# A fused RWKV-6 and SiLU kernel: the first layer of units 3 to 11 by eleven half-products in place of twelve

## The chip, the cores and the metric

The kernel runs on one core of a Trainium2 chip, everything in float32. The metric is the time on the device in microseconds, the median over runs. Engines are called TensorE (PE; PEld is its weight load), VectorE (DVE), ScalarE (ACT), GpSimd (POOL) and SyncE (SP, which issues the DMAs).

## The reference

An attention block of the RWKV-6 kind is followed by two matrix products with a SiLU between them:

```python
batch, n_heads, seq, head_dim = (4, 8, 768, 48)
for t in range(S):
    kt, vt, rt, wt = (k[:, :, t], v[:, :, t], r[:, :, t], w[:, :, t])
    cur = np.einsum('bhd,bhe->bhde', u[None] * kt, vt)
    y[:, :, t] = np.einsum('bhd,bhde->bhe', rt, state + cur)
    state = wt[:, :, :, None] * state + np.einsum('bhd,bhe->bhde', kt, vt)
...
x = y.transpose(0, 2, 1, 3).reshape(B * S, H * D)      # 3072 x 384
h = x @ w_in                                           # 384 x 2048
g = h * (1.0 / (1.0 + np.exp(-h)))
out = g @ w_out                                        # 2048 x 384
```

## The kernel before

The work is cut into twelve units: 128 time steps (`L`) of two batches (`NB`), so 256 tokens (`TU`). Units 0, 2, 4 and so on hold batches 0 and 1, the others batches 2 and 3. A unit goes through the attention part, then the first layer, then the second layer.

**Attention.** Within a unit the recurrence is computed by levels of blocks that double in length (1, 2, 4 up to 64). `turn` transposes w, r and k into rows of time (VectorE, L356). `grow_keys` (GpSimd, L630) and `grow_queries` or `prepare` (VectorE, L612 and L767) multiply keys and queries by the decays of the blocks. `burst(i, l)` makes the score products of two levels at once on TensorE (L688), from the queries before and after a `prepare`. `keep_level` moves them into `score` (VectorE L706 for short blocks, ScalarE L788 for the long ones). `block_bonus` and `block_sum` compute the scores inside blocks of eight tokens on GpSimd (L487) and VectorE (L521), from the tile `tokens_rk`, which `load_rk` fetches. The sums go through DRAM (`block_move`: `kept`, then `spare`) and are spread by ScalarE (`block_spread`, L548 and L550) and written into `score` by VectorE (`block_write`, L557). After level 6, `go_on(i, 6)` multiplies the queries once more (L612). Then TensorE computes `turn_apart` (L807), `y_state` (L831, reads those queries, and L838), `y_values` (L852) and `update` (L892). `move_x` (L918) carries the result through ten DMAs into the tile `xt`, in three chunks of 128 input columns; there is one buffer of it.

**First layer.** `up(i, m)`, m from 0 to 7, multiplies `xt` by 256 columns of `w_in`: two blocks of 128 columns, three chunks each, with all 256 tokens as the moving side (L1000). ScalarE applies the SiLU from PSUM into `gt` (L1009).

**Second layer.** From unit 1 on it takes seven products of halves in place of eight (a scheme of Winograd's kind). `sums(i, m)` makes the four sums of `gt` on VectorE (L1048, tile `temps`), `quarter(i, which)` the seven products (L1066), with VectorE adding the parts from PSUM (L1075). `weight_sums` made the four sums of `w_out` once, early.

**Order.** All instructions are written in an order fixed by hand (`manual_schedule`); each engine works through its own in that order. From unit 3 on, one round of the main loop handles unit i's attention, unit i-1's first layer and unit i-2's second layer: `mix(i)` gives the attention in eleven groups (13 for i = 3), and `room` says how many steps of the layers follow each group. For i from 4 on it is

```python
steps = downs(i - 2) + ups(i - 1)          # 7 quarters, then 8 first-layer steps
room = (2, 1, 2, 2, 1, 1, 1, 2, 1, 1, 1)
```

So quarters 3 and 4 follow group 2 (key and query products of level 2), quarters 5 and 6 follow group 3 (`prepare(i, 3)`), and the first-layer steps follow group 4 (`burst(i, 3)`, block sums, `block_move`, `load_rk`) to group 10. Group 8 holds `burst(i, 5)`, `keep_level` 5 and 6 and `go_on(i, 6)`; group 9 the first four `block_bonus` steps of unit i+1; group 10 `turn_apart` to `update`, the transposes of unit i+1's w and k, and one of the four `sums`. `move_x(i - 1)` stands in group 1. After unit 11's attention, `downs(10)`, `ups(11)` and `downs(11)` follow with nothing between.

**Loads.** w, r and k of a unit are fetched by 16 DMAs each (`load_blocks`, L123) into `raw`, which has two slots, one for even and one for odd units. SP issues all DMAs of the kernel in their written order. In round i, r of unit i+1 and w and k of unit i+2 are fetched, spread over groups 2 to 10.

PSUM: `p_h` and `p_o` have two buffers each, `p_m` and `p_sc` two banks each.

Of the kernel before, what the change touches and what calls it, by code (L numbers as in the profile page):

```python
# [8 lines left out]
F32 = mybir.dt.float32  # L9
# [6 lines left out]
ALU = mybir.AluOpType  # L16
# [22 lines left out]
def kernel(  # L39
# [17 lines left out]
    NB = 2  # L57
# [56 lines left out]
    def load_blocks(i, name, g):  # L114


        n, b0 = units[i]
        src, t0 = {"w": w, "r": r, "k": k}[name], n * L + g * 32
        room = raw[:, i % NSLOT, WRK[name]].rearrange("p b h d -> p (b h d)").rearrange("p (q g d) -> p q g d", q=Q, d=32)
        for e in range(2):  # L120
            for a in range(2):
                d0, d1 = a * 32, min(D, a * 32 + 32)
                nc.sync.dma_start(out=room[(2 * e + a) * 32:(2 * e + a + 1) * 32, :, g, 0:d1 - d0],  # L123
                                  in_=src[b0:b0 + NB, e::2, t0:t0 + 32, d0:d1].rearrange("b q t d -> t (b q) d"))
# [217 lines left out]
    def turn(i, b, name):  # L342
        dst = {"w": tw, "r": tr, "k": tk}[name]
        if i not in dst:
            rows = NX if name == "k" else Q
            t = pt.tile([128, rows, L], F32, name="t" + name, bufs=2 if name == "r" else 1)
            dst[i] = [t] if name == "w" else t
        t = dst[i][0] if name == "w" else dst[i]
        if i < NTOK:
            if (i, b, name) not in turned:  # L350
                turn_in(i, b, name)
            turn_out(i, b, name, t)
        else:
            row0 = b * NP + (NP if name == "k" else 0)
            to, back = t[:, row0:row0 + NP, :], name == "k" and b == 1
            nc.vector.transpose(out=to[:, ::-1, ::-1] if back else to,  # L356
                                in_=raw[:, i % NSLOT, WRK[name], b].rearrange("p h d -> p (h d)"))

    turned = {}

# [569 lines left out]
    def mix(i):  # L930

        ahead = i + 1 < len(units)

        def at(now, *steps):
            return steps if now else ()

        def bonus_steps(j, *steps):
            return [(block_bonus, j, x) for x in steps]

        def sum_steps(j, *steps):  # L940
            return [(block_sum, j, x) for x in steps]

        def turns(j):
            return [*both(turn, j, "w"), (product, j, 0), *both(turn, j, "k")]

        def start(j):
            return [*[(product, j, l) for l in range(1, NL)], (grow_own, j, 1)]

        end = [[*at(ahead, *bonus_steps(i + 1, 0, 1, 2, 3))],
               [*at(i < len(units) - NB, (turn_apart, i), (turn_k, i)), (y_state, i), *both(y_values, i), *at(ahead, *turns(i + 1)),  # L950
                (sums, i - 1, FH // 2 - 2), *both(update, i), *at(not ahead, (move_x, i))]]
        if i < NPAIR:
            groups = [[*both(turn, i, "w"), (product, i, 0)],
                      [*both(turn, i, "k"), (odd_ones, i)], [*both(turn, i, "r"), (start_levels, i), (prepare_keys, i, 1)],
                      [(prepare, i, 1), *[(product, i, l) for l in range(1, NL)]],
                      [(burst, i, 1), (keep_level, i, 1)],
                      [(keep_level, i, 2), (go_on, i, 2)],
                      [(prepare, i, 3), (reverse_v, i), (bonus, i, 0), (bonus_sum, i, 0)],
                      [(bonus, i, 1), (burst, i, 3), (keep_level, i, 3), (bonus, i, 2)],
                      [(keep_level, i, 4), (go_on, i, 4), (bonus_sum, i, 1), (load_rk, i + 1), (load_u,)],  # L960
                      [(prepare, i, 5), (make_block_mask,), (bonus_spread, i), (bonus_write, i)],
                      [(burst, i, 5), (keep_level, i, 5), (keep_level, i, 6), (go_on, i, 6)], *end]
        else:
            groups = [[*both(turn, i, "r"), (grow_own, i, 0)], [*start(i), *sum_steps(i, 0, 1), *bonus_steps(i, 4, 5), (move_x, i - 1)],
                      [(odd_keys, i, 2), (grow_keys, i, 2, False), (grow_queries, i, 2), *sum_steps(i, 2)],
                      [(prepare, i, 3), *bonus_steps(i, 6, 7)],
                      [(burst, i, 3), (keep_level, i, 3), *sum_steps(i, 3, 4), (block_move, i), *at(ahead, (load_rk, i + 1))],
                      [(keep_level, i, 4), (go_on, i, 4)],
                      [(prepare, i, 5), (reverse_v, i)],
                      [(block_spread, i), (block_write, i)],  # L970
                      [(burst, i, 5), (keep_level, i, 5), (keep_level, i, 6), (go_on, i, 6)], *end]

        loads = [*at(i >= NPAIR - 1 and ahead, *block_loads(i + 1, "r")), *at(i + NSLOT < len(units), *block_loads(i + NSLOT, "wk"))]
        if i + 1 < len(units):
# [17 lines left out]
    FH, DH = FC // 2, DM // 2  # L992
    NFIRST = 2 * PW // (2 * TU)

    def up(i, m):
        p_h = ps.tile([128, 2, TU], F32, name="p_h", bufs=2)
        for a in range(2):
            f = 2 * m + a
            for c in range(KC):
                nc.tensor.matmul(p_h[:, a, :], lhsT=w_in_sb[:, c, f * 128:(f + 1) * 128], rhs=xt[i][:, c, :],  # L1000
                                 start=(c == 0), stop=(c == KC - 1))
# [7 lines left out]
        nc.scalar.activation(out=gt[i, m], in_=p_h, func=AF.Silu)  # L1009

    def out_room(b):

# [28 lines left out]

    def sums(i, m):

        lower, upper = (gt[i, x].rearrange("p a (b t) -> p b a t", b=NB) for x in (m, m + FH // 2))
        s1, s2, s3, s4 = (quarters[:, x, 2 * m:2 * m + 2, :] for x in range(4))
        for out, one, two, op in ((s1, lower[:, 1], upper[:, 1], ALU.add), (s2, s1, lower[:, 0], ALU.subtract),
                                  (s3, lower[:, 0], lower[:, 1], ALU.subtract), (s4, upper[:, 0], s2, ALU.subtract)):
            nc.vector.tensor_tensor(out=out, in0=one, in1=two, op=op)  # L1048

    ob, partial = {}, {}  # L1050
# [1 line left out]
    def quarter(i, which):  # L1052

        n, b0 = units[i]

        def g(b, half):
            return lambda f: gt[i, (f + half * FH) // 2][:, f % 2, b * L:(b + 1) * L]

        def s(x):
# [22 lines left out]

    def ups(i):

        steps = [[(up, i, m)] for m in range(FC // 2)]
# [92 lines left out]
    for step in downs(len(units) - 2) + ups(len(units) - 1) + downs(len(units) - 1):  # L1178
        do(*step)


# [28 lines left out]
```

## Time and profile before

| | |
|---|---|
| time, median of 3 runs | 595.06 us (594.48 to 595.62) |
| span of the profiled execution (its own time is given by this span alone) | 593.4 us, clock 1.000 |
| TensorE busy | 584.0 us (98%) |
| VectorE busy | 411.1 us (69%) |
| GpSimd busy | 351.6 us (59%) |
| ScalarE busy | 225.5 us (38%) |
| first layer, L1000, 1152 records | 259.1 us |
| quarters, L1066 (three groups, 1212 records) | 88.1 + 86.5 + 30.4 us |

A float32 matmul shows as two records, each with its own weight load. Busy time of a group of matmuls counts the time that at least one of them was under way; the time of one record is its latency, and the distance between the starts of two is what a record costs. In the timeline, a row merges instructions of one kind that follow each other: its start, its length, and their count.

### The profile page before, as it was taken

The numbers are of one execution on the slowest core, as the hardware profiler recorded it, in microseconds if no ns is written. First come the engines' busy times: TensorE is split into PE (matmuls) and PEld (weight loads), VectorE is DVE, ScalarE is ACT, GpSimd is POOL, SyncE is SP. The second block draws the span as 40 slices with busy tenths as digits, with TensorE's granted clock in tenths as the row PEclk, the third lists the DMA queues.
The fourth block names the chain that finished last, engine by engine and source line by source line (L and its number), as shares of the span: only waits on it lengthen the run. The fifth ranks groups of instructions, "written<-read, shape, count | busy, mean of one in ns | idle before, by whom it ended". The sixth has DMA issues, their size and how long they took to land.

```text
span 593.4 us, 14697 instructions
## 1 busy us (share of the span) xinstructions
PE 584.0 (98%) x5766; PEld 523.3 (88%) x5766; DVE 411.1 (69%) x716; ACT 225.5 (38%) x495; POOL 351.6 (59%) x415
## 2 busy tenths in 40 slices
PE   8989999999999999999999999999999999999997
PEld 8767876799899899899899899899889889889997
DVE  7979789889785596695695695696686586542041
ACT  5689684531521530530540450351361351350110
POOL 5989778358467378468467577477477577500000
PEclk9999999999999999999999999999999999999999
DMA  9957785343543643642643643643543530101000
GB/s 224 312 131 212 153 234 77 47 87 65 110 62 52 139 64 55 137 61 52 140 64 55 132 62 52 136 63 56 126 67 54 118 51 27 38 1 29 27 1 27
DMA packets 203221, 53.40 MB, mean 90 GB/s; under 512 B 186768, under 2 KB 194960, under 8 KB 203152
## 3 DMA queue, kind: packets, MB, share of 16 engines
q1 hardware_dynamic: 201568, 51.88, 43.1%
q8 instruction: 45, 0.74, 0.6%
q10 hardware_dynamic: 1584, 0.59, 0.5%
q14 instruction: 24, 0.20, 0.1%
HBM read 43.21 MB, written 5.24 MB: 82 GB/s over the span
## 4 chain that ended last, share of the span: by engine, by line
PE 75%; SPq 11%; DMA 5%; POOL 3%; DVE 3%; issue 2%; ACTq 0%; POOLq 0%; DVEq 0%
PE p_h L1000 33%; PE p_o L1066 30%; SPq L123 6%; PE p_m L1022 4%; PE p_sc L688 2%; DMA tokens_w<-in_w_dram 2%; PE p_m L852 2%; POOL w_in_sb L255 2%; DMA vq<-in_v_dram 2%; PE p_m L831 1%; PE p_m L688 1%; SPq L206 1%; SPq L107 1%; SPq L918 1%; POOL tk L630 1%
## 5 line engine op out<-in xcount | busy, mean ns | idle before, releaser
L1000 PE MATMUL p_h<-xt,w_in_sb 128*128 128x256 f32 x1152 | 259.1, 382 | 1.7 <-POOL w_in_sb L255 1.5
L1000 PEld LDWEIGHTS p_h<-xt,w_in_sb 128*128 128x128 f32 x1152 | 215.7, 190 | 32.5 <-POOL w_in_sb L255 2.4
L1009 ACT ACTIVATE gt<-p_h 128x512 f32<-128x512 f32 x90 | 53.5, 596 | 179.8 <-PE p_h L1000 179.6
L630 POOL TENSOR_TENSOR tk<-tk,tw 128x256 f32<-128x256 f32 x128 | 95.8, 770 | 36.9 <-issue 21.9
L487 POOL TENSOR_TENSOR ruk<-tokens_rk 128x768 f32<-128x768 f32 (+1 forms) x32 | 51.6, 1622 | 63.3 <-DMA tokens_rk<-in_k_dram 27.7
L1066 PE MATMUL p_o<-own,temps 128*128 128x192 f32 x528 | 88.1, 326 | 0.3 <-DVE temps L1075 0.3
L1066 PEld LDWEIGHTS p_o<-own,temps 128*128 128x128 f32 x528 | 86.0, 190 | 0.7 <-DVE temps L1075 0.6
L1066 PE MATMUL p_o<-w_out_sb,gt 128*128 128x192 f32 x508 | 86.5, 326 | 0.0
L1066 PEld LDWEIGHTS p_o<-w_out_sb,gt 128*128 128x128 f32 x508 | 83.4, 190 | 0.8 <-DVE partial L1075 0.2
L1048 DVE TENSOR_TENSOR temps<-gt 128x256 f32<-128x256 f32 x84 | 49.5, 590 | 26.6 <-ACT gt L1009 26.3
L612 DVE TENSOR_TENSOR tr<-tr,tw 128x512 f32<-128x512 f32 x61 | 57.4, 941 | 13.1 <-PE p_m L688 12.7
L402 POOL TENSOR_TENSOR tw<-tw 128x256 f32<-128x256 f32 (+6 forms) x83 | 39.6, 478 | 36.8 <-DVE tw L356 32.9
L600 ACT COPY tk<-tk 128x256 f32<-128x256 f32 x52 | 21.0, 403 | 103.9 <-POOL tk L630 83.6
L706 DVE COPY_PREDICATED score<-mask,p_sc 128x512 f32<-128x512 int8 x42 | 31.2, 796 | 3.0 <-PE p_sc L688 2.8
L1075 DVE TENSOR_TENSOR partial<-p_o,partial 128x192 f32<-128x192 f32 x33 | 11.7, 355 | 29.6 <-PE p_o L1066 29.6
L1066 PE MATMUL p_o<-w_out_sb,temps 128*128 128x192 f32 x176 | 30.4, 326 | 0.0
L1075 DVE TENSOR_TENSOR temps<-p_o,partial 128x192 f32<-128x192 f32 x22 | 7.9, 358 | 32.0 <-PE p_o L1066 25.8
L521 DVE TENSOR_REDUCE block_sums<-ruk 128x4 f32<-128x192 f32 (+1 forms) x48 | 24.2, 546 | 7.1 <-POOL ruk L487 7.1
L1066 PEld LDWEIGHTS p_o<-w_out_sb,temps 128*128 128x128 f32 x176 | 28.9, 190 | 0.0
L857 ACT COPY yt<-p_m 48x512 f32<-48x512 f32 x40 | 23.2, 580 | 13.8 <-PE p_m L852 13.1
L1048 DVE TENSOR_TENSOR temps<-temps,gt 128x256 f32<-128x256 f32 x43 | 27.4, 638 | 1.5
L688 PEld LDWEIGHTS p_sc<-tr,tk 48*64 48x64 f32 x960 | 17.3, 134 | 12.0 <-issue 7.9
(182 smaller groups left out, 794.7 us busy)
## 6 DMA issues: line engine op xcount, KB each, us to landing
w_out_sb<-in_moe_w_in_dram SPq DMA_DIRECT2D x6, 768.0 KB, 7.1
w_out_sb<-in_moe_w_out_dram SPq DMA_DIRECT2D x4, 768.0 KB, 5.1
own<-in_moe_w_out_dram SPq DMA_DIRECT2D x4, 768.0 KB, 6.6
tokens_rk<-in_r_dram SPq DMA_DIRECT2D x8, 384.0 KB, 4.4
tokens_rk<-in_k_dram SPq DMA_DIRECT2D x8, 384.0 KB, 5.3
tokens_w<-in_w_dram SPq DMA_DIRECT2D x8, 384.0 KB, 6.3
xt<-yt SPq DMA_DIRECT2D x60, 48.0 KB, 2.0
raw<-in_w_dram SPq DMA_DIRECT2D x80, 32.0 KB, 2.1
```

The costliest lines, as they stand in the source:

```text
L123: nc.sync.dma_start(out=room[(2 * e + a) * 32:(2 * e + a + 1) * 32, :, g, 0:d1 - d0], in_=src[b0:b0 + NB, e::2, t0:t0 + 32, d0:d1].rearran ...
L402: engine.tensor_tensor(out=up, in0=t[:, :, 0::2], in1=t[:, :, 1::2], op=ALU.mult)
L487: mul = lambda out, one, two: nc.gpsimd.tensor_tensor(out=out, in0=one, in1=two, op=ALU.mult)
L521: add = lambda out, have: nc.vector.tensor_reduce(out=out, in_=have, axis=mybir.AxisListType.X, op=ALU.add)
L612: nc.vector.tensor_tensor(out=odd, in0=odd, in1=tw[i][l][:, :, 0::2][:, :, :, None].to_broadcast([128, Q, L >> (l + 1), c]), op=ALU.mult)
L630: nc.gpsimd.tensor_tensor(out=out, in0=have, in1=odd_products(i, l, b, *blocks), op=ALU.mult)
L688: nc.tensor.matmul(to, lhsT=tk[i][rows, X[l % 2] + p, x * 64:(x + 1) * 64], rhs=have, start=True, stop=True)
L706: nc.vector.copy_predicated(out=dst, mask=masks[l][:, :, None].to_broadcast([128, NB, NP, ni, c]), data=sc[e].rearrange("p (b q) (i c) -> ...
L1000: nc.tensor.matmul(p_h[:, a, :], lhsT=w_in_sb[:, c, f * 128:(f + 1) * 128], rhs=xt[i][:, c, :], start=(c == 0), stop=(c == KC - 1))
L1009: nc.scalar.activation(out=gt[i, m], in_=p_h, func=AF.Silu)
L1048: nc.vector.tensor_tensor(out=out, in0=one, in1=two, op=op)
L1066: nc.tensor.matmul(p, lhsT=left(f), rhs=right[:, f, :], start=(f == 0), stop=(f == FH - 1))
```

## The change

For units 3 to 11 (`NFAST` = 3) the first layer is cut in halves: the 2048 output columns into two halves of 1024, the 256 tokens into two of 128 (one per batch). The first two chunks of the 384 input columns and these halves form a 2x2 by 2x2 product, done in seven products of halves (p1 to p7); the third chunk is done plainly, in four products that ride along (a13, a23, and n1 for the last). That is eleven products where there were twelve. Each product goes over four blocks of 128 columns per step, with 128 tokens as the moving side, so a half step is four matmuls of 128x128 weights by 128 columns.

The sums that the seven products need are kept in PSUM where products follow each other: three places, x in `p_h`, y and z in `p_o`. A place's running sum is copied or added out before the next product is added onto it. `first_layer` does one or more of the products of one half of the 1024 columns, with what follows each: a ScalarE copy of the running sum into `gt`, or a VectorE addition of PSUM onto `gt` and then a SiLU in place, or the SiLU straight from PSUM. `sums_of_x` makes the four differences of `xt` (and overwrites one chunk of it) on VectorE, after quarter 4 of the round. `in_weight_sums` makes the sums of `w_in` once: three in round 3, one in round 4. Two of them live in slot 1 of `raw` where w and r were, so from unit 4 on w and r use slot 0 alone, and w of unit i+1 is fetched in round i.

`sums` handles two pieces of 128x512 per sum instead of four of 128x256: the first follows step 4 of the first layer (group 7), the second the last step; the one in group 10 falls away for these units.

```diff
+    def slot(i, name):
+        return 0 if i >= NPAIR and name != "k" else i % NSLOT
...
-                (sums, i - 1, FH // 2 - 2), *both(update, i), *at(not ahead, (move_x, i))]]
+                *at(i - 1 < NFAST, (sums, i - 1, FH // 2 - 2)), *both(update, i), *at(not ahead, (move_x, i))]]
...
-        loads = [*at(i >= NPAIR - 1 and ahead, *block_loads(i + 1, "r")), *at(i + NSLOT < len(units), *block_loads(i + NSLOT, "wk"))]
+        loads = [*at(i >= NPAIR and ahead, *block_loads(i + 1, "w")), *at(i >= NPAIR - 1 and ahead, *block_loads(i + 1, "r")),
+                 *at(i + NSLOT < len(units), *block_loads(i + NSLOT, "k"))]
...
+    def in_weight_sums(which):
+        out, one, two, op = ((in_sums[0], a21, a22, ALU.add), (in_sums[1], in_sums[0], a11, ALU.subtract),
+                             (in_sums[2], a12, in_sums[1], ALU.subtract), (a21, a11, a21, ALU.subtract))[which]
+        nc.vector.tensor_tensor(out=out, in0=one, in1=two, op=op)
+
+    def sums_of_x(i):
+        (b11, b12), (b21, b22), (b31, b32) = (tuple(xt[i][:, c, b * L:(b + 1) * L] for b in range(NB)) for c in range(KC))
+        d1, d2, d4, d3 = x_sums
+        for out, one, two in ((d1, b12, b11), (d2, b22, d1), (b12, b22, b12), (d4, b21, d2), (d3, b31, b32)):
+            nc.vector.tensor_tensor(out=out, in0=one, in1=two, op=ALU.subtract)
+
+    def first_layer(i, half, *names):
...
+        for name in names:
+            place, first, last, pairs = {
+                "p1": ("x", True, True, [(a11, b11)]), "p6": ("x", False, True, [(s2, d2)]), "p7": ("x", False, True, [(a21, b12), (a23, b32)]),
+                "p4": ("x", False, True, [(a22, d4), (a23, d3)]), "p5": ("y", True, True, [(s1, d1)]),
+                "p3": ("y", False, True, [(s4, b22), (a13, b32)]), "p2": ("z", True, False, [(a12, b21)]),
+                "n1": ("z", False, True, [(a13, b31)])}[name]
...
+            for n, (left, right) in enumerate(pairs):
+                for q in range(4):
+                    f = (4 * half + q) * 128
+                    nc.tensor.matmul(p[:, q, :], lhsT=left[:, f:f + 128], rhs=right, start=first and n == 0 and q == 0,
+                                     stop=last and n == len(pairs) - 1 and q == 3, skip_group_check=True)
...
+            if name in ("p1", "p6", "p5"):
+                nc.scalar.copy(out=g(*{"p1": (0, 0), "p6": (0, 1), "p5": (1, 1)}[name]), in_=p)
+            elif name in ("n1", "p7", "p3"):
+                to = g(*{"n1": (0, 0), "p3": (0, 1), "p7": (1, 1)}[name])
+                nc.vector.tensor_tensor(out=to, in0=p, in1=to, op=ALU.add)
+                nc.scalar.activation(out=to, in_=to, func=AF.Silu)
+            elif name == "p4":
+                nc.scalar.activation(out=g(1, 0), in_=p, func=AF.Silu)
...
     def ups(i):
+        if i >= NFAST:
+            order = (((0, "p1"), (0, "p5"), (0, "p2")), ((0, "p6"), (0, "n1"), (1, "p1")), ((0, "p7"), (0, "p3")),
+                     ((0, "p4"), (1, "p5"), (1, "p2")), ((1, "p6"), (1, "n1")), ((1, "p7"),), ((1, "p3"),), ((1, "p4"),))
+            made = [[(first_layer, i, half, name) for half, name in step] for step in order]
+            made[4].append((sums, i, 0))
+            made[-1].append((sums, i, 1))
+            return made
...
+        if i - 1 >= NFAST:
+            steps[4].append((sums_of_x, i - 1))
         if i == NTOK + 1:
             groups[4].insert(1, (weight_sums, 3))
+            for which, place in enumerate((6, 8, 9)):
+                groups[place].append((in_weight_sums, which))
+        if i == NFAST + 1:
+            steps[1].append((in_weight_sums, 3))
...
+    steps[4].append((sums_of_x, len(units) - 1))
```

More of the change, by code (lines that the diff above doesn't have):

```diff
@@ L118, in load_blocks @@
         src, t0 = {"w": w, "r": r, "k": k}[name], n * L + g * 32
-        room = raw[:, i % NSLOT, WRK[name]].rearrange("p b h d -> p (b h d)").rearrange("p (q g d) -> p q g d", q=Q, d=32)
+        room = raw[:, slot(i, name), WRK[name]].rearrange("p b h d -> p (b h d)").rearrange("p (q g d) -> p q g d", q=Q, d=32)
         for e in range(2):
@@ L356, in turn @@
             nc.vector.transpose(out=to[:, ::-1, ::-1] if back else to,
-                                in_=raw[:, i % NSLOT, WRK[name], b].rearrange("p h d -> p (h d)"))
+                                in_=raw[:, slot(i, name), WRK[name], b].rearrange("p h d -> p (h d)"))
     turned = {}
@@ L992 @@
     FH, DH = FC // 2, DM // 2
+    NFAST = 3
     NFIRST = 2 * PW // (2 * TU)
@@ L1009, in up @@
         nc.scalar.activation(out=gt[i, m], in_=p_h, func=AF.Silu)
+    HALF = DF // 2
+    whole_w = raw[:, 1].rearrange("p x b h d -> p x (b h d)")
+    in_sums = [whole_w[:, WRK["r"]], const.tile([128, HALF], F32, name="in_sum"), whole_w[:, WRK["w"]]]
+    a11, a12, a13 = (w_in_sb[:, c, 0:HALF] for c in range(KC))
+    a21, a22, a23 = (w_in_sb[:, c, HALF:DF] for c in range(KC))
+    x_sums = [spare[:, at + x * L:at + (x + 1) * L] for x in range(3)] + [const.tile([128, L], F32, name="x_sum")]
@@ new lines, with g @@
+    chain = {}
+    def first_layer(i, half, *names):
+        (b11, b12), (b21, b22), (b31, b32) = (tuple(xt[i][:, c, b * L:(b + 1) * L] for b in range(NB)) for c in range(KC))
+        d1, d2, d4, d3 = x_sums
+        s1, s2, s4 = in_sums
+        for name in names:
[4 more added lines that the diff above has]
+                "n1": ("z", False, True, [(a13, b31)])}[name]
+            if first:
+                pool, tag = (ps, "p_h") if place == "x" else (second[0], "p_o")
+                chain[place, half] = pool.tile([128, 4, L], F32, name=tag, bufs=2)
+            p = chain[place, half]
+            for n, (left, right) in enumerate(pairs):
[3 more added lines that the diff above has]
+                                     stop=last and n == len(pairs) - 1 and q == 3, skip_group_check=True)
+            def g(x, b):
+                if (i, x, b, half) not in gt:
+                    gt[i, x, b, half] = pt.tile([128, 4, L], F32, name="gt", bufs=FC // 2)
+                return gt[i, x, b, half]
+            if name in ("p1", "p6", "p5"):
[6 more added lines that the diff above has]
+                nc.scalar.activation(out=g(1, 0), in_=p, func=AF.Silu)
@@ L1042, in sums @@
     def sums(i, m):
[L1044 to L1047, printed above, removed]
+        if i >= NFAST:
+            lower, upper = ([gt[i, x, b, m] for b in range(NB)] for x in range(2))
+            lower, upper = ([t[:, :, :] for t in have] for have in (lower, upper))
+            s1, s2, s3, s4 = (quarters[:, x, 4 * m:4 * m + 4, :] for x in range(4))
+        else:
+            lower, upper = (gt[i, x].rearrange("p a (b t) -> p b a t", b=NB) for x in (m, m + FH // 2))
+            lower, upper = ([have[:, b] for b in range(NB)] for have in (lower, upper))
+            s1, s2, s3, s4 = (quarters[:, x, 2 * m:2 * m + 2, :] for x in range(4))
+        for out, one, two, op in ((s1, lower[1], upper[1], ALU.add), (s2, s1, lower[0], ALU.subtract),
+                                  (s3, lower[0], lower[1], ALU.subtract), (s4, upper[0], s2, ALU.subtract)):
             nc.vector.tensor_tensor(out=out, in0=one, in1=two, op=op)
@@ L1056, in g @@
         def g(b, half):
+            if i >= NFAST:
+                return lambda f: gt[i, half, b, f // 4][:, f % 4, :]
             return lambda f: gt[i, (f + half * FH) // 2][:, f % 2, b * L:(b + 1) * L]
@@ L1083, in ups @@
     def ups(i):
+        if i >= NFAST:
+            order = (((0, "p1"), (0, "p5"), (0, "p2")), ((0, "p6"), (0, "n1"), (1, "p1")), ((0, "p7"), (0, "p3")),
[4 more added lines that the diff above has]
+            return made
         steps = [[(up, i, m)] for m in range(FC // 2)]
@@ L1177 @@
             steps = steps[count:]
-    for step in downs(len(units) - 2) + ups(len(units) - 1) + downs(len(units) - 1):
+    steps = downs(len(units) - 2) + ups(len(units) - 1) + downs(len(units) - 1)
+    steps[4].append((sums_of_x, len(units) - 1))
+    for step in steps:
         do(*step)
```

## The prediction

> **What bounds the kernel now.** I read the page first: shares of the span, then the chain.
>
> ```profile
> PE 584.0 (98%) x5766; PEld 523.3 (88%) x5766; DVE 411.1 (69%) x716; ACT 225.5 (38%) x495; POOL 351.6 (59%) x415
> PE p_h L1000 33%; PE p_o L1066 30%; SPq L123 6%; PE p_m L1022 4%; PE p_sc L688 2%; DMA tokens_w<-in_w_dram 2%; PE p_m L852 2%; POOL w_in_sb L255 2%; DMA vq<-in_v_dram 2%; PE p_m L831 1%; PE p_m L688 1%; SPq L206 1%; SPq L107 1%; SPq L918 1%; POOL tk L630 1%
> ```
>
> TensorE is busy throughout, and a third of the chain is the first layer (L1000), the line that changes. Then the timeline of TensorE over one steady round of `mix` (i = 7, 306.8 to 352.6 us; rounds 6 to 9 each last 45.8): no gap anywhere.
>
> ```profile
> 312.02 7.96 PE L1066 MATMUL p_o<-own,temps 128*128 128x192 f32 x48
> 326.21 13.22 PE L1000 MATMUL p_h<-xt,w_in_sb 128*128 128x256 f32 x60
> 340.45 5.45 PE L1000 MATMUL p_h<-xt,w_in_sb 128*128 128x256 f32 x24
> ```
>
> So every product saved is time, as long as nobody makes TensorE wait. The timelines of VectorE and GpSimd in the stretch before `y_state` (346.45) show who could:
>
> ```profile
> 336.32 2.50 DVE L557 COPY_PREDICATED score<-spare 128x1024 f32<-128x1024 int8 x2
> 340.61 2.30 DVE L612 TENSOR_TENSOR tr<-tr,tw 128x512 f32<-128x512 f32 x1 [1.79 <-PE p_m L688]
> 342.83 1.22 DVE L1048 TENSOR_TENSOR temps<-gt 128x256 f32<-128x256 f32 x1
> 344.09 1.12 DVE L1048 TENSOR_TENSOR temps<-temps,gt 128x256 f32<-128x256 f32 x1
> 345.13 0.41 DVE L1048 TENSOR_TENSOR temps<-gt 128x256 f32<-128x256 f32 x1
> ```
>
> ```profile
> 337.78 2.69 POOL L487 TENSOR_TENSOR ruk<-tokens_rk 128x768 f32<-128x768 f32 x1 [3.86 <-DMA tokens_rk<-in_k_dram]
> 340.55 1.81 POOL L487 TENSOR_TENSOR ruk<-ruk,u_bc 128x768 f32<-128x768 f32 x1
> 342.32 1.46 POOL L487 TENSOR_TENSOR spare<-tokens_rk 128x384 f32<-128x384 f32 x1
> 343.85 1.07 POOL L487 TENSOR_TENSOR tokens_rk<-tokens_rk,tokens_w 128x384 f32<-128x384 f32 x1
> ```
>
> VectorE and GpSimd take turns, instruction by instruction. L612 takes 0.67 alone (330.01) and 2.30 here, ending at 342.91, 0.6 after the GpSimd instruction that began at 340.55 ended. The sum L1048 takes 0.41 alone, 1.22 and 1.12 here. GpSimd pays too: its first product takes 2.69 instead of 1.81 because L557 holds on until 338.8. VectorE instructions that read PSUM (L1075, 0.36) are not slowed. In the before kernel this costs nothing: L612 makes the queries that `y_state` reads, and is done 3.5 us ahead of it.
>
> **PE's part.** Steady spacing, by differences of those rows: (13.22-5.45)/36 = 0.216 us per record of 256 columns, (7.96-5.36)/16 = 0.1625 per record of 192 (5.36 is the 32-record row at 306.82). 64 columns are 0.0533, so 128 columns stream in 0.109. No first-layer matmul of 128 columns exists before. The weight loads then come as close as they can; their own pace shows where 16-column matmuls hide nothing:
>
> ```profile
> 57.47 0.86 PEld L570 LDWEIGHTS p_m<-own_sums,partial 128*128 128x128 f32 x7
> ```
>
> (0.86-0.19)/6 = 0.112. I take 0.112 per record (bounds 0.109 and, if the two interfere by a tenth, 0.123). A unit had 48 matmuls in 96 records: 96 x 0.216 = 20.7 us. It gets 11 products x 8 = 88 matmuls, 176 records: 176 x 0.112 = 19.7. Gain 1.0 us a unit (1.5; or a loss of 0.9), nine units: -9.5 us (-13 to +8). So an eleventh-for-twelfth (8%) shrinks to 5%, since weights are loaded twice as often.
>
> [...]
>
> **Cost one: the sums of half 0 now stand ahead of L612.** This decides my sign. Clock from `burst(i,3)` = 0 (325.12 before). TensorE after: burst to 1.1, restart 0.2, 128 records 14.3: n1 of half 1 ends at 15.6; `burst(i,5)` to 16.7; 32 records and a restart to 20.45; `turn_apart` 0.6; `y_state` would start at 21.1 (before: 21.3).
> ScalarE now copies `spare` (five copies, 1.25) behind the Silu of p3: p3 ends 10.2, VectorE's add 0.65 (128x192 from PSUM starts the next 0.27 later, 320 more columns at 1 ns), Silu 0.6, copies: 12.8. VectorE's shuffle 0.25 and the two L557 copies 2.4: 15.5 (before 13.7). Then, in order: add of n1 to 16.3; four sums of 128x512, 0.6 each as L612 alone starts the next: 18.7; only then L612: 19.3. Alone that is 1.8 us in time. But GpSimd's four products, 5.5 us when alone, start when `tokens_rk` lands, at 12.7 as before (the same DMAs on SP's queue). Taking turns, the three sets end one after the other: 12.7 + 5.5 + 2.4 + 2.4 + 0.6 = 23.6, 2.5 late; if L557 goes ahead and only GpSimd waits, 1.2 late; ScalarE's `keep_level` copies (3.7 us, L788), behind n1's Silu, agree: 20.0 + 3.7. I take 2.0 us of PE waiting (0 to 2.6).
>
> **Cost two: `sums_of_x`.** Five 128x128 subtractions (0.2 each alone) enter VectorE between the additions of quarter 4 and `prepare(i,3)` (L767, 0.92), which the second half of `burst(i,3)` reads. Queued behind them are also the additions of quarters 5 and 6; their PSUM buffers are needed only 2 us after the burst. Two things hold them: `xt` must have landed, and GpSimd's four key products (L630, 0.6 each) and two bonus products (1.81 each) run just then, one turn per subtraction.
>
> ```profile
> 314.94 6.28 SPq L918 DMA_DIRECT2D xt<-yt  x10
> 321.27 4.03 SPq L123 DMA_DIRECT2D raw<-in_r_dram  x8
> ```
>
> `xt`'s last transfer is issued at 320.6 and lands 1.9 later, 322.5; quarter 4's additions end at 320.65. So VectorE waits some 2 us, then does the last subtraction and L767: 323.5 to 326 with one or two GpSimd turns of 1.81, against 325.6 when the burst wants it. In round 4 `xt` lands at 186.6 and the burst is at 186.9: 1 us late. I take 0.6 us (0 to 2.1).
>
> **What is hidden.** The six additions and three more ScalarE copies per half lie beside the 20 us of products. The product that adds onto a PSUM sum waits for the copy of that sum; each has at least one other product (0.9 us) between, a copy takes 0.6: nothing, or 0.3 if ScalarE is late. Weight sums, four of 128x1024 (1.2 each): in round 3 VectorE has gaps of 0.6 and 3.0 us before it is needed; 0 to 1 in all, taken as 0.3. Loads of w and r now share one slot and are issued one round ahead: SP has the same number of issues, w's last half goes out by clock 14 and its transpose is due at 22; nothing, and 2 us a round if SP were late. Its backlog does not move.
>
> **Sum.** Rounds 4 to 10 pay both costs: 7 x (2.0 + 0.6) = 18.2. Round 11 has no bonus for a next unit, and the last unit runs alone: neither pays. -9.5 + 18.2 + 0.3 = +9.0. The profiled span 593.4 becomes 602.4; the median lies 1.7 above the span, so 595.06 becomes 604. With 1.45 a round it is 596, with 3.5 it is 610; 614 takes both costs near their ends.
>
> **Rivals.**
> 1. *GpSimd does not delay the sums* (the turns fall otherwise, or its products start later, behind a later `tokens_rk`). Then L612 is 1.8 us early, cost one is nil, and at most cost two stays: 595.06 - 9.5 = 585.6, up to 590. For: VectorE alone has the time, and TensorE is the only full engine. Against: the turns above, alike in rounds 6 to 10. This is faster.
> 2. *SP's chain becomes the bound.* From the write of `block_sums` (328.90) to the last `xt` issue of the next round SP issues almost without pause (38.3 us), then 1.9 to land, last subtraction and L767 1.2, additions 0.6, keep and block sums 3: 45 to 46.3, against TensorE's 44.7. If this alone binds, rounds stay near 45.8 and only round 11 and the end gain: about 594 to 598. It decides once TensorE loses under 1.1 us a round. For: SP idles only some 4 us a round. Against: it follows VectorE, which cost one already makes later.
> 3. *Weight loads interfere at 128 columns* beyond a tenth: over 0.123 a record, +8 us or more and both costs, above 614. Against: the 0.112 and 0.1625.
>
> **Numbers.** Forecast 0.60, near 604 (its own range 596 to 614); rival 1 0.22; rival 2 0.12, of which a third is within 0.2%, about what a measurement here can tell from no change; rival 3 0.06. Faster 0.22, same 0.04, slower 0.74. The range 587 to 614 reaches into rival 1 and leaves out its best end, rival 3 and the worst pile-up.
>
> **What would show it.** Right: records of 128 columns 0.112 apart; a gap in TensorE before the state products (`y_state`), put down to VectorE's `tr` multiply or ScalarE's score copies, 1 to 2.6 us in each of rounds 4 to 10 and none in round 11; sums of 128x512 that take over 1 us where GpSimd is in L487; a smaller gap in the middle of `burst(i,3)`. Wrong: rounds of 44.7 with `y_state` following `turn_apart` at once (rival 1); rounds near 45.8 with a wait for `xt` (rival 2); a spacing above 0.12 (rival 3).

## The result, and the profile after

The changed kernel takes 613.89 us (median of 4 runs, 608.84 to 615.64) against 594.81 (594.48 to 595.62): a ratio of 1.0305, 95% interval 1.0259 to 1.035. The profiled execution took 615.42 us, with a span of 613.6 and a mean granted clock of 0.989. The page, busy time by engine and the chain that ended last:

```profile
PE 584.4 (95%) x6486; PEld 546.9 (89%) x6486; DVE 478.1 (78%) x747; ACT 254.8 (42%) x549; POOL 361.8 (59%) x415
PE 45%; DVE 19%; SPq 14%; DMA 11%; issue 6%; POOL 3%; ACT 1%; DVEq 0%; POOLq 0%; ACTq 0%
```

TensorE is as busy as before in microseconds although it does less work (part of it ran on half a clock, below), and its share fell from 98% to 95%: the 20 us are time in which it stands. VectorE is 19% of the chain. The timeline of TensorE in round 8 (start, length, what is done, in brackets the idle time before it and who ended it):

```profile
379.44 0.69 PE L692 MATMUL p_sc<-tr,tk 48*64 48x64 f32 x32
380.85 0.69 PE L692 MATMUL p_m<-tr,tk 48*64 48x64 f32 x32 [0.71 <-DVE tr L771]
...
390.51 1.06 PE L1056 MATMUL p_h<-spare,w_in_sb 128*128 128x128 f32 x8
391.40 1.06 PE L1056 MATMUL p_h<-x_sum,w_in_sb 128*128 128x128 f32 x8
392.29 1.06 PE L1056 MATMUL p_o<-spare,raw 128*128 128x128 f32 x8
...
400.82 0.84 PE L811 MATMUL p_sc<-ident,tk 48*128 48x48 f32 x16
404.02 1.13 PE L835 MATMUL p_m<-tr,state 48*48 48x128 f32 x32 [2.36 <-DVE tr L616]
```

Three things: a hole in the middle of `burst(i,3)`, whose halves start 1.41 apart instead of 0.5; the first layer (now L1056) in rows of eight records that start 0.893 apart, 0.1117 per record; and the wait of `y_state` (now L835) for the queries' multiply (now L616). The waits of TensorE over the whole run (us in total, times, longest) show that the two waits come in seven rounds each:

```profile
PE p_m L835 <- DVE tr L616: 14.0, 7, 3.1
PE p_m L692 <- DVE tr L771: 4.3, 7, 0.7
...
PE p_sc L811 <- ACT score L792: 1.4, 2, 0.8
```

How the wait of `y_state` came about, in the timelines of VectorE and GpSimd in round 7:

```profile
346.08 4.86 DVE L561 COPY_PREDICATED score<-spare 128x1024 f32<-128x1024 int8 x2
350.84 0.67 DVE L1068 TENSOR_TENSOR gt<-p_o,gt 128x512 f32<-128x512 f32 x1
351.43 0.89 DVE L1116 TENSOR_TENSOR temps<-gt 128x512 f32<-128x512 f32 x1
352.36 1.38 DVE L1116 TENSOR_TENSOR temps<-temps,gt 128x512 f32<-128x512 f32 x1
...
354.87 0.68 DVE L616 TENSOR_TENSOR tr<-tr,tw 128x512 f32<-128x512 f32 x1
```

```profile
345.13 1.83 POOL L491 TENSOR_TENSOR ruk<-tokens_rk 128x768 f32<-128x768 f32 x1 [2.79 <-DMA tokens_rk<-in_k_dram]
347.04 2.73 POOL L491 TENSOR_TENSOR ruk<-ruk,u_bc 128x768 f32<-128x768 f32 x1
```

The two predicated copies took 2.50 before and take 4.86 now: GpSimd's first product got in ahead of one of them, its second ahead of the other. Then come an addition and the four sums, and only then the multiply. Not every round is like this one: in rounds 5, 6 and 8 to 10 the copies took 4.12 to 4.14, one product's turn, and GpSimd held up the sums more instead (1.71, 1.37 and 1.50 for the first three in round 8, where 0.68 is the time alone).

Behind the wait the clock fell. The windows of round 8 (us; busy time of PE, PEld, DVE, ACT and POOL with their instructions; granted TensorE clock, DMA share, GB/s):

```profile
395.00:398.00 3.00, 3.00 (x82) 2.81 (x81) 3.00 (x2) 0.59 (x1) 2.92 (x2) 1.00 0.29 36
401.50:404.00 2.50, 0.16 (x5) 0.04 (x2) 2.50 (x4) 0.92 (x3) 0.62 (x1) 1.00 0.81 153
404.00:408.00 4.00, 3.98 (x92) 3.92 (x94) 3.48 (x6) 3.35 (x7) 1.63 (x3) 0.72 0.42 51
```

In the trace's record of the clock this is a stretch of 3.41 us at 0.5, from 405.7. There are four such stretches among the rounds (211.2, 405.7, 453.5, 504.7), each behind such a wait; the profiled execution of the kernel before has none there. Rounds, from the start of quarter 0 to the next one's:

| round | 4 | 5 | 6 | 7 | 8 | 9 | 10 | 11 | last unit |
|---|---|---|---|---|---|---|---|---|---|
| before | 45.78 | 46.53 | 45.78 | 45.78 | 45.78 | 45.78 | 44.44 | 44.44 | 38.92 |
| after | 48.66 | 48.07 | 48.31 | 47.46 | 49.78 | 49.55 | 48.90 | 44.31 | 38.52 |
| stretch at half clock | yes | | | | yes | yes | yes | | |

The four runs of the changed kernel differ by 6.8 us, and their mean clocks differ with them: clocks of 0.989, 0.989, 0.994 and 0.997 go with 615.42, 615.64, 612.37 and 608.84 us.

### The profile page after: what moved, and what is told of

Read it like the earlier page. It is cut to its first block, busy times and chain, and to the rows that moved or that the text cites. A ratio compares the mean times of both kernels' runs of the same rounds, so it can differ in the third digit from the quotient of the medians.

```text
span 613.6 us, 16240 instructions
## 1 busy us (share of the span) xinstructions
PE 584.4 (95%) x6486; PEld 546.9 (89%) x6486; DVE 478.1 (78%) x747; ACT 254.8 (42%) x549; POOL 361.8 (59%) x415
## 4 chain that ended last, share of the span: by engine, by line
PE 45%; DVE 19%; SPq 14%; DMA 11%; issue 6%; POOL 3%; ACT 1%; DVEq 0%; POOLq 0%; ACTq 0%
PE p_o L1136 19%; PE p_h L1056 7%; SPq L127 7%; PE p_o L1056 4%; PE p_h L1006 4%; DVE temps L1116 3%; PE p_m L1084 3%; DVE spare L1034 3%; DMA tokens_w<-in_w_dram 3%; PE p_m L856 2%; DMA vt<-in_v_dram 2%; SPq L922 2%; DVE score L710 2%; DMA vq<-in_v_dram 2%; PE p_m L835 2%
## 5 line engine op out<-in xcount | busy, mean ns | idle before, releaser
L1006 PE MATMUL p_h<-xt,w_in_sb 128*128 128x256 f32 x288 | 66.1, 384 | 1.7 <-POOL w_in_sb L259 1.6
L1006 PEld LDWEIGHTS p_h<-xt,w_in_sb 128*128 128x128 f32 x288 | 53.6, 190 | 10.0 <-POOL w_in_sb L259 2.4
L1069 ACT ACTIVATE gt<-gt 128x512 f32<-128x512 f32 x54 | 33.8, 630 | 62.2 <-DVE gt L1068 62.1
L1065 ACT COPY gt<-p_h 128x512 f32<-128x512 f32 x36 | 20.9, 581 | 87.2 <-PE p_h L1056 87.2
L1056 PE MATMUL p_o<-xt,w_in_sb 128*128 128x128 f32 x432 | 57.1, 275 | 0.0
L1056 PE MATMUL p_h<-xt,w_in_sb 128*128 128x128 f32 x432 | 54.3, 279 | 0.0
L1056 PEld LDWEIGHTS p_o<-xt,w_in_sb 128*128 128x128 f32 x432 | 52.6, 192 | 0.0
L616 DVE TENSOR_TENSOR tr<-tr,tw 128x512 f32<-128x512 f32 x61 | 51.9, 850 | 0.5
L1056 PEld LDWEIGHTS p_h<-xt,w_in_sb 128*128 128x128 f32 x432 | 50.4, 192 | 1.1
L1116 DVE TENSOR_TENSOR temps<-gt 128x512 f32<-128x512 f32 (+1 forms) x48 | 43.2, 901 | 3.1 <-ACT gt L1015 1.6
L1068 DVE TENSOR_TENSOR gt<-p_o,gt 128x512 f32<-128x512 f32 x36 | 24.6, 684 | 18.6 <-PE p_o L1056 18.6
L561 DVE COPY_PREDICATED score<-spare 128x1024 f32<-128x1024 int8 x16 | 33.1, 2118 | 0.3
```

The costliest lines, as they stand in the source:

```text
L561: nc.vector.copy_predicated(out=score[:, i % NSC, e].rearrange("p (b q) (i s) -> p b q i s", b=NB, s=BLK), mask=block_mask[:, :, None].to_ ...
L616: nc.vector.tensor_tensor(out=odd, in0=odd, in1=tw[i][l][:, :, 0::2][:, :, :, None].to_broadcast([128, Q, L >> (l + 1), c]), op=ALU.mult)
L1056: nc.tensor.matmul(p[:, q, :], lhsT=left[:, f:f + 128], rhs=right, start=first and n == 0 and q == 0, stop=last and n == len(pairs) - 1 an ...
L1069: nc.scalar.activation(out=to, in_=to, func=AF.Silu)
```

## The experiments

The theory was the prediction's: the four sums of half 0, behind copies that take turns with GpSimd, hold up the multiply (cost one), `sums_of_x` the second half of the burst (cost two). Rivals: ScalarE's copies into `score`, behind n1's SiLU, hold `y_state` just as long; the cause is GpSimd's work at that place alone; the clock is a cost of its own; and the products themselves are dearer than 0.112 a record.

**e1: the half-0 sums one step later, behind the multiply.**

```diff
-            made[4].append((sums, i, 0))
+            made[5].append((sums, i, 0))
```

> The first of the two sets of sums (half 0) is moved behind go_on(i, 6) and p7 of half 1 on VectorE; nothing else changes. Theory A (the order on VectorE: the sums stand ahead of the tr multiply that y_state reads): the multiply ends 3 to 4 us earlier, the gap of 2.5 us before y_state goes, 613.9 falls by 7 x 2.5 and by the stretches at half clock: about 592 to 598. Theory B (ScalarE: the SiLU of n1 waits for VectorE's addition, which stands behind the two predicated copies, and the 12 copies of keep_level stand behind that SiLU): in the changed kernel's round 7 those copies end at 355.76 and the multiply at 355.55, so the gap stays within 0.3 us of what it was: 612 to 614.5.

Measured: 611.35 us, ratio 1.026 (1.0233 to 1.0288). Timelines of VectorE and ScalarE in round 7, then TensorE's waits:

```profile
351.07 0.89 DVE L616 TENSOR_TENSOR tr<-tr,tw 128x512 f32<-128x512 f32 x1
```

```profile
351.18 0.63 ACT L1069 ACTIVATE gt<-gt 128x512 f32<-128x512 f32 x1 [3.45 <-DVE gt L1068]
351.72 2.13 ACT L792 COPY score<-p_sc 32x128 f32<-32x128 f32 x8
353.88 1.52 ACT L792 COPY score<-p_m 64x256 f32<-64x256 f32 x4
```

```profile
PE p_m L835 <- ACT score L792: 3.3, 8, 0.8
PE p_sc L811 <- ACT score L792: 3.1, 4, 0.8
```

Counted from `burst(i,5)` (347.94 here, 348.53 in after) the multiply is done 3.0 us sooner, at 4.0 in place of 7.0; but TensorE now waits for the copies, which end at 7.5 (7.2 in after). There are two holders, and the second was hidden by the first. Rounds 5 to 7, which have no stretch at half clock, took 47.5 to 47.7 in place of 47.5 to 48.3; the profile still has three stretches, one of them of double length. In the last unit the round fell from 38.52 to 37.90: sums placed that early cost 0.6 there too.

**e2: GpSimd's first four bonus products behind `update`.**

```diff
-        end = [[*at(ahead, *bonus_steps(i + 1, 0, 1, 2, 3))],
+        end = [[],
...
-                ... *both(update, i), *at(not ahead, (move_x, i))]]
+                ... *both(update, i), *at(ahead, *bonus_steps(i + 1, 0, 1, 2, 3)), *at(not ahead, (move_x, i))]]
```

> GpSimd's four bonus products of the next unit are issued after update instead of before turn_apart; nothing is left out. Theory A and B both say that the two predicated copies then take 2.4 us again instead of 4.9, n1's addition comes as TensorE ends it, and y_state starts without a gap: minus 7 x 2.5 and the half-clock stretches (4 x 1.7 us), that is 590, if GpSimd's later work has room. GpSimd then makes the keys 4 to 5 us later; they were ready about 4 us ahead of burst(i,3), so 0 to 1.5 us a round may come back there: 590 to 601. If VectorE's own order were the cause and not the turns with GpSimd, the gap would stay at 2 us or more: above 608.

Measured: 610.07 us, 1.0254 (1.0226 to 1.0281). The wait before `y_state` is gone in every round; in its place the quarters wait, in round 7 here (VectorE, then TensorE):

```profile
324.43 1.14 DVE L525 TENSOR_REDUCE block_sums<-ruk 128x4 f32<-128x192 f32 x4 [3.25 <-POOL ruk L491]
```

```profile
325.88 2.87 PE L1136 MATMUL p_o<-w_out_sb,gt 128*128 128x192 f32 x16 [1.99 <-DVE partial L1145]
```

GpSimd delivers the products later, VectorE stops 3.25 us at the reduction of them, and the additions that free a quarter's PSUM place stand behind it. So without GpSimd's turns there is no cost one; but its work has to be done somewhere, and the one other place that was tried had its own wait, and four stretches at half clock among its rounds.

**e3: 14 identity transposes on TensorE ahead of `y_state`.** They add work into a `p_h` buffer that nothing reads.

```diff
-  ... (turn_apart, i), (turn_k, i)), (y_state, i),
+  ... (turn_apart, i), (turn_k, i)), *at(i > NPAIR - 1 and ahead, (fill, 14)), (y_state, i),
```

> 14 transposes of the identity (1.5 us) into a free PSUM buffer stand before y_state in rounds 4 to 10, where TensorE sits idle for 1.9 to 3.4 us. If the stretches of 3.4 us at half clock come from these idle times, they go, and the time falls by up to 4 x 1.7 us less 0.5 us in rounds whose gap is short: 607 to 610, and the runs lie closer together than 608.8 to 615.6. If the clock drops for another reason, it stays at 4 stretches and the time at 613 to 615.

Measured: 612.58 us, 1.0286 (1.0272 to 1.0301), a miss by 3 us. What was expected of the clock came true: no stretch at half clock behind 110 us where after has four, and the runs lie within 0.8 us (612.05 to 612.84) where those of the changed kernel spread over 6.8. But the rounds took 47.3 to 49.0, not the 47.5 to 48.3 of the undisturbed rounds of after: the filled rounds are no shorter than undisturbed ones, and only a part of what the clock took came back. A part of the rest shows in the trace: in rounds 4 and 7, where after needed only 2.43 and 2.30 us from `turn_apart` to `y_state`, the fill made it 3.30 and 3.19, 1.8 us in all. The remainder is not settled.

**e4: the kernel before, with the first layer of units 3 to 11 cut into matmuls of 128 columns,** nothing else changed.

```diff
-                nc.tensor.matmul(p_h[:, a, :], lhsT=w_in_sb[:, c, f * 128:(f + 1) * 128], rhs=xt[i][:, c, :], ...
+                for b in range(NB if i >= 3 else 1):
+                    part = slice(b * L, (b + 1) * L) if i >= 3 else slice(0, TU)
+                    nc.tensor.matmul(p_h[:, a, part], lhsT=w_in_sb[:, c, f * 128:(f + 1) * 128], rhs=xt[i][:, c, part], ...
```

> The kernel before, with each first-layer matmul of units 3 to 11 cut into two of 128 columns with the same weights: 192 records a unit in place of 96, no other work. If the pace at 128 columns is that of the weight loads (0.112), a unit costs 21.5 us in place of 20.7: 9 x 0.75 = 6.8, so 601.6 (range 600 to 603). If loads and streams did not overlap (0.22 a record): over 750. If 128 columns cost 0.109, 597.

Measured: 602.03 us, 1.0111 (1.0096 to 1.0125). The steady rounds went from 45.78 to 46.49, so 96 matmuls of 128 columns cost 0.71 us more than 48 of 256. TensorE's timeline:

```profile
329.07 13.67 PE L1002 MATMUL p_h<-xt,w_in_sb 128*128 128x128 f32 x120
342.67 0.69 PE L688 MATMUL p_sc<-tr,tk 48*64 48x64 f32 x32
```

13.60 us for 120 records and a change of kind: the pace is settled, and the products are not dearer than forecast.

**e5: `sums_of_x` behind `prepare(i,3)`.**

```diff
-            steps[4].append((sums_of_x, i - 1))
+            groups[3].insert(1, (sums_of_x, i - 1))
```

> sums_of_x stands behind prepare(i, 3) on VectorE instead of ahead of it; nothing else. If cost two is what the prediction says (the burst waits for the multiply behind the five subtractions), the hole of 0.7 to 1.0 us inside burst(i, 3) goes in rounds 4 to 11, and the time falls by 8 x 0.85 = 6 to 8 us: 606 to 608. Rival: the hole was cover for something else (xt's landing, the copies behind the burst), and comes back as a wait of p5 for its difference or before y_state: 611 to 614.

Measured: 617.16 us, 1.0368 (1.0335 to 1.0402), slower than after where 606 to 608 was expected. The hole in the burst is gone, and the two rounds that have no half-clock stretch in either kernel took 47.32 in place of 48.07 (round 5) and 43.57 in place of 44.31 (round 11); but this run had six stretches, three of them of double length, and rounds with one took 48.9 to 50.1. So cost two is real, 0.75 us a round, and removing it alone was paid back by the clock.

**e6: `block_spread`'s five ScalarE copies earlier, before the SiLUs of p7 and p3,** so that VectorE's predicated copies run ahead of GpSimd's products.

```diff
-                      [(prepare, i, 5), (reverse_v, i)],
-                      [(block_spread, i), (block_write, i)],
+                      [(prepare, i, 5), (reverse_v, i), (spread_copies, i)],
+                      [(spread_turn, i), (block_write, i)],
```

> Only the five ScalarE copies of block_spread stand earlier, ahead of the SiLUs of p7 and p3 of half 0, so that VectorE's two predicated copies come before GpSimd's bonus products. By the turns: copies 2.4 instead of 4.9, n1's addition as TensorE ends it, ScalarE's keep_level copies end near 20.7; the four sums still take turns with two or three GpSimd products, so the multiply ends near 22 against 21.1: the gap before y_state falls from 2.5 to about 1 us. Minus 7 x 1.5 and some of the half-clock stretches: 599 to 605. If the collision of the predicated copies were not the cause: 612 to 615.

Measured: 604.22 us, 1.0146 (1.0115 to 1.0178), as expected. VectorE's and GpSimd's timelines in round 7 (10 lines were added above, so L561 is L571):

```profile
339.37 2.52 DVE L571 COPY_PREDICATED score<-spare 128x1024 f32<-128x1024 int8 x2
```

```profile
340.98 2.54 POOL L491 TENSOR_TENSOR ruk<-tokens_rk 128x768 f32<-128x768 f32 x1 [3.42 <-DMA tokens_rk<-in_k_dram]
```

Now GpSimd waits for the copies, not they for it. The gap before `y_state` fell from about 2.6 to 1.1 (1.31 at most up to round 9), rounds to 46.7 to 46.9, and no stretch at half clock followed any of them.

**e7: n1's SiLU behind ScalarE's `score` copies, the half-0 sums behind the multiply,** both holders at once.

```diff
-                nc.scalar.activation(out=to, in_=to, func=AF.Silu)
+                if (name, half) != ("n1", 1):
+                    nc.scalar.activation(out=to, in_=to, func=AF.Silu)
...
-            made[4].append((sums, i, 0))
+            made[5].insert(0, (late_silu, i))
+            made[5].append((sums, i, 0))
```

> The SiLU of n1 (half 1) stands behind keep_level's copies on ScalarE, and half 0's sums behind go_on(i, 6) on VectorE; the predicated copies stay late and collide. Both holds on y_state are taken away at once: copies end near 20, multiply near 21.2 by the turns, against 21.1. The gap is then under 0.3 us, no half-clock stretch is left: 613.9 - 17.5 - 6 = 590 to 595. If the gap has a third holder (score's predicated copies, p7's copy), it stays over 1 us: above 603.

Measured: 603.21 us, 1.0137 (1.0119 to 1.0155), above the 590 to 595 that were expected. `y_state` no longer waits, and a third holder stands behind the two, in the waits of TensorE:

```profile
PE p_sc L896 <- ACT kq L819: 7.3, 6, 1.5
```

`update` waits for the key copies of `turn_k`, queued on ScalarE behind the SiLUs. Together with e2 this shows what cost one needs: GpSimd's products at that place, which e2 takes away, and the sums and the SiLU ahead of the two holders, which e7 moves; either edit ends the wait of `y_state`.

**e8 to e11: the pieces put together.** e8 has e5, e6 and e7 in one. e9 also puts the three SiLUs of half 1 (n1, p7, p3) behind the key copies. e10 also puts the half-0 sums behind p3's addition (`made[6]`). e11 is e10 with `sums_of_x` split: two subtractions behind quarter 5's addition, three behind quarter 6's.

```diff
+  ... (turn_apart, i), (turn_k, i)), *at(i - 1 >= NFAST, (late_silus, i - 1)), (y_state, i),      # e9, e10, e11
...
-            made[5].append((sums, i, 0))
+            made[6].append((sums, i, 0))                                                          # e10, e11
...
-            groups[3].insert(1, (sums_of_x, i - 1))
+            steps[5].append((sums_of_x, i - 1, 0))                                                # e11
+            steps[6].append((sums_of_x, i - 1, 1))
```

> All three moves: SiLU of n1 and half 0's sums late, block_spread early, sums_of_x behind prepare(i, 3). By the prediction's sum only TensorE's gain is left: 595.1 - 9.5 = 585.6, up to 589, rounds of 44.7 to 45.2. Rival (SP's chain from block_sums to xt binds next): rounds stay at 45.5 to 46.3, 593 to 598.

> As e8, but all three SiLUs of half 1 (n1, p7, p3) stand behind turn_k's copies on ScalarE in rounds 4 to 11. In e8 update waits 0.9 to 1.6 us a round for those copies (kq), which stand behind the SiLU of p3. If that is the last hold, rounds of 46.1 become 45.1 to 45.4 and the time 590 to 592, below the kernel before (595). Rival (SP's chain from block_sums to xt, some 45 to 46.3 us a round): rounds stay at 45.7 to 46.2, with a wait for sums_of_x: 594 to 596.

> As e9, and half 0's sums one step later, behind p3's addition on VectorE, so that p3's place in PSUM and its SiLU come 2.5 us earlier, while the transposes of the next unit come 0.3 us later. If VectorE's queue ahead of the transposes binds (GpSimd waits for them), 0 to 1 us slower than e9; if p3's SiLU does (sums of half 1 and quarter 2), 0 to 2 us faster: 589 to 593.

> The last kernel (SiLUs, spread copies and sums of half 0 moved) with one more edit: of the five subtractions of `sums_of_x`, the first two now stand behind the addition of quarter 5 and the other three behind that of quarter 6, in place of all five ahead of both. What is on trial is whether the only wait left in its rounds, p5 waiting 0.45 to 1.6 us for the PSUM place that quarter 5's addition frees, was one of order. If it was: p5 follows p1 at once, rounds near 45.0 where they were 45.0 to 45.75, no half-clock stretch behind this wait, and 589 to 593, below the kernel before (594.9). If the subtractions bind by themselves (they wait for xt, landed near 320.2 in round 7, and take turns with GpSimd's two products of 1.81), the wait moves on to p2, p6 or p7, of about the same size, and the time stays at 594 to 596.

| | us | ratio (95% interval) | rounds 4 to 9 | what TensorE still waits for |
|---|---|---|---|---|
| e8 | 596.39 | 1.0021 (1.0011 to 1.0031) | 45.7 to 46.7 | key copies, up to 1.3 |
| e9 | 597.22 | 1.0033 (1.0021 to 1.0046) | 45.1 to 46.5, one 48.5 | p5's PSUM place, up to 1.6; one half-clock stretch |
| e10 | 594.44 | 0.9992 (0.9976 to 1.0008) | 45.0 to 45.75, one 48.6 | the same, four times, up to 1.6; one stretch |
| e11 | 596.62 | 1.0038 (1.0021 to 1.0054) | 45.66 to 46.4 | p4 behind VectorE's additions; quarters |

e10 is level with the kernel before; none beats it, and none reached its forecast (585.6 to 589, 590 to 592, 589 to 593, and 589 to 593 again). In e10 a round without the wait of p5 takes 45.03 to 45.07, 0.7 less than before; its quarters still wait some 0.3 (in round 5 the burst starts 18.63 after quarter 0, against 18.30 in round 7 of the kernel before), so the products alone would give the 44.7 that was forecast. What is left of its waits, on VectorE and TensorE in round 7:

```profile
321.36 1.91 DVE L1044 TENSOR_TENSOR spare<-xt,spare 128x128 f32<-128x128 f32 x1
323.19 1.91 DVE L1044 TENSOR_TENSOR x_sum<-xt 128x128 f32<-128x128 f32 x1
325.02 0.35 DVE L1161 TENSOR_TENSOR ob<-p_o,partial 128x192 f32<-128x192 f32 x1
```

```profile
325.42 1.16 PE L1066 MATMUL p_o<-spare,raw 128*128 128x128 f32 x8 [0.45 <-DVE ob L1161]
```

Two subtractions of 128 columns wait out a GpSimd product each, 1.9 us in place of the 0.28 that they take alone, and quarter 5's addition, which frees p5's place, stands behind them. e11 took that order away, and its rivals' case came true: p5 follows at once, but the last subtraction ends 3.6 us after the start of `burst(i,3)` (325.19) in place of 2.4 (322.72 in e10), what stands behind it on VectorE is late as well, and p4 waits:

```profile
324.95 0.73 DVE L1045 TENSOR_TENSOR spare<-xt,spare 128x128 f32<-128x128 f32 x1 [1.69 <-DMA xt<-yt]
```

```profile
335.84 1.16 PE L1067 MATMUL p_h<-spare,w_in_sb 128*128 128x128 f32 x8 [0.36 <-DVE gt L1079]
```

So what is left stands on VectorE: in e10 it is busy for 454.8 us, 44 more than in the kernel before, and takes turns with GpSimd besides. But in round 7 its subtractions also wait for the transfers of `xt`, 0.86 us in e10 and 1.69 in e11, the chain that the second rival of the prediction named. No run tells the two apart.

## Why the prediction was right, and where it was not

The forecast, 604.0 with 587 to 614, was slower for the reason that it named; the time lies 10 us above the number and inside the range by 0.1 us, with two of the four runs above it. That the range held is luck: its upper end was meant for both costs near their ends, and the time came so high by a clock term that is not in the sum. Step by step:

- **The pace of 128 columns: right.** 0.112 taken, 0.1117 measured, and e4 shows it apart from the rest. The full gain appears where nothing waits: the last unit takes 37.90 in place of 38.92 in the kernels whose half-0 sums stand late.
- **Cost one: right in place and in kind, too small in size.** Counted from `burst(i,3)`, the multiply was to end at 23.6 if the turns fall one after the other; in round 7 it ended at 355.55 - 331.98 = 23.57. That match is chance: in rounds 5, 6 and 8 to 10 the turns fell otherwise, and it ended at 24.2 to 24.5. I then took 2.0 a round, below that case. The gaps before `y_state`, as distances of starts less the usual spacing, sum to 17.1 us in rounds 4 to 10, against 7 x 2.0 = 14. "ScalarE's copies agree" was right as well (e1), but I used it only as support: they were a second holder, done 0.2 us behind the multiply in rounds 4 and 7 and 1.4 ahead of it in rounds 5, 6 and 8 to 10, so that moving the sums alone could not free the place, and a third stood behind it (e7).
- **Cost two: right in place, a little small.** The holes come to 5.7 us, against 4.2. They stand in rounds 5 to 11, not 4 to 10: for round 4 I said 1 us, and there is none; for round 11, none, and it has 0.74. `sums_of_x` there takes turns with two GpSimd products as in every round (two subtractions of 1.90, at 524.20 and 526.03). I had let them end with the "bonus for a next unit", but they belong to the unit itself. So round 11 gained 0.13 in place of 1.0. `xt`, the other reason that I gave, did not hold VectorE in rounds 7 and 8: the first two subtractions follow the addition without a pause.
- **Weight sums, loads, additions and copies: right at little.** Round 3, for which 0.3 was taken, takes 47.18 in both kernels. In round 4, where the fourth weight sum stands on VectorE (1.22 us), `burst(i,3)` starts 18.69 after quarter 0 in place of 18.29, which is 0.4 that I did not have.
- **The clock: missing in the sum.** Four stretches of 3.41 us at half speed cost up to 1.7 us each. In rounds 8 and 9 the way from `y_state` to the next quarter 0 took 6.91 and 6.84 in place of the 5.40 of round 6; rounds 4 and 10 give 1.6 and 1.4 against 7 and 11, so some 6.0 in all. No row of before could show them, since it has no such gap; but a sum that puts 2 us gaps into a TensorE that never stood should have given them a bound. This term is the largest part of the 10 us.
- **The last unit pays nothing: wrong by 0.6**, since its half-0 sums stand ahead of additions that it waits for (38.52 against 37.90).

Round 5 of the kernel before had a wait of its own among the quarters (46.53 in place of 45.78), which after does not have. Together: -9.5 + 17.1 + 5.7 + 6.0 + 0.6 + 0.4 - 0.8 = 19.5, against 20.2 more in the span; the 0.7 is not settled. Without the clock the same profile would be near 609.4, 5.4 above the forecast.

Of the rivals, the first (GpSimd does not delay) is refuted by L561's 4.86; the second (SP's chain) did not show in after, where TensorE is never released by `xt`, and stays open for e8 to e11 as said; the third is refuted by 0.1117. Why the two copies took both turns in round 7 and only 4.13 us in round 8 was not tried; GpSimd's first product began 13.15 after the burst in the one and 14.30 in the other.

## What to carry to other kernels

Where one engine is full, saved products are worth their share only if the additions that replace them fit into the order of the engines that feed it: for each new instruction, ask what stands behind it in its queue, and list every holder of the next product with its due time, since freeing the latest one uncovers the next. A gap on a TensorE that never stood can cost more than its length: here a clock term, some 6.0 us in all, came on top in four of eight rounds. And a subtraction of 0.28 us on VectorE can cost a whole GpSimd instruction (1.9 us) where the two run side by side, so ask of each short one what GpSimd does just then. That few long sums would do better than five short ones was not tried.

## What the runs showed of the hardware that was not expected

- **The clock.** After gaps of TensorE of 1.0 + 0.96, 2.59, 2.60 and 3.40 us (distances of starts, after's rounds 4, 8, 9 and 10) the granted clock was 0.5 for 3.41 us; after others of 2.57 and 2.59 (rounds 5 and 6) and of 0.88 + 0.95 (round 7) it stayed at 1.0, as it did behind the gaps of 1.06 to 1.74 in e6. In e9 and e10 one gap of 1.6 us each was followed by a stretch, seen in e9 in the pace of the next rows, 1.46 and 1.70 in place of 0.89 (TensorE's timeline):

```profile
281.23 1.66 PE L1066 MATMUL p_o<-spare,raw 128*128 128x128 f32 x8 [1.61 <-DVE ob L1161]
282.69 1.92 PE L1066 MATMUL p_o<-xt,w_in_sb 128*128 128x128 f32 x8
284.39 1.41 PE L1066 MATMUL p_h<-spare,in_sum 128*128 128x128 f32 x8
```

  Gaps of 2.57 to 2.60 us stand on both sides, so their length alone does not tell which of them brings a stretch. What decides was not shown: no run varied the length or the place of a gap by itself.
- **Turns.** VectorE's multiplies (0.67 alone, 2.30 beside GpSimd, in the kernel before), sums of 128x512 (0.68 and up to 1.71, after's round 8) and subtractions of 128x128 (0.28 and 1.91, after's round 7) from SBUF alternate with GpSimd's by whole instructions in these traces, and so do predicated copies (2.50 when they start first, 4.86 between two GpSimd products, 2.52 again when e6 put them ahead). VectorE additions of 128x192 that read PSUM kept their 0.35 beside GpSimd (before, at 317.72; e10, at 325.02), and a reduction of 128x768 its 0.94 (e2, at 318.92).
